# Reading the 384 moving columns of the MLP products as two interleaved halves

## The chip, the cores and the metric

The kernel runs on one core of one Trainium2 chip. The metric is the device time of one execution in microseconds (us), here the median of several runs. A core has a matrix engine (PE, TensorE), whose loads of the stationary operand are shown as PEld, a vector engine (DVE), an activation engine (ACT), a third elementwise engine (POOL, GpSimd), and SP, which issues DMAs.

## What is computed

An attention with random features, then a two-layer MLP with SiLU, then a gated three-matrix MLP, on 2304 tokens of 512 features, all in float32:

```python
def _moe_ref(x, w_in, w_out):                 # 512 -> 2048 -> 512
    h = x @ w_in
    g = h * (1.0 / (1.0 + np.exp(-h)))
    return g @ w_out

def _moe2_ref(x, w_gate, w_val, w_out):       # 512 -> 1536 -> 512
    g = x @ w_gate
    silu = g * (1.0 / (1.0 + np.exp(-g)))
    return (silu * (x @ w_val)) @ w_out

x = attention(q, k, v, omega)                 # (2304, 512)
out = _moe2_ref(_moe_ref(x, w_in, w_out), w_gate, w_val, w_out2)
```

## The kernel before, in words

Activations are kept transposed: features on the 128 partitions, tokens along the free dimension. Tokens are cut into three blocks (`s`, NSB = 3) of two halves of N = 384 tokens each. There are four MLP stages, in this order: up 0 (`w_in`), down 0 (`w_out`), up 1 (`w_gate`, `w_val`), down 1 (`w_out2`). Each is computed with seven block products of a Strassen scheme (`PROD`, `ORDER`) in place of eight; sums and differences of blocks are made by ACT, DVE and POOL. Each float32 operand is split into a high and a low float32r part, and each product is taken as high by high, high by low and low by high, three matmuls.

The up stages run in `up_phase`. Its inner function `products` (line 1085) issues one block product: six matmuls at line 1097, each with a stationary 128x128 piece of a weight (`cut(l, j * P, P)`) and 384 moving columns of an activation block (`cut(r, j * N, N)`), into one PSUM bank `ps[b][:, :N]`. The down stages run in `down_phase`; for each pair of feature blocks it issues twelve matmuls at line 1472, again 128x128 by 384 columns (`b` is the high or low activation piece). The result of a stage is drained from PSUM by ACT (lines 1114, 1138, 1413) and DVE (1155, 1171, 1427), goes through DRAM tensors (`g_d`, `x2_d`), is loaded again, and is split for the next stage (lines 1331, 1335).

Each engine's instructions stand in an order fixed when the program is written: `Op`, `Stream`, `flush` and `need` place work by a planner's cost table, in which a matmul of 384 columns counts as `MM = 0.1735` us. No cost in that table is touched by the change. The attention stage (matmuls at lines 751, 795, 811, 842, 867) comes first; nine matmuls on zeros at line 734 precede it, of the same 128x128 by 384 form as those of the MLPs.

On the host, `kernel` lays out the inputs, launches once, and transposes `out_0` (512 x 2304) at the end.

Of the kernel before, what the change touches and what calls it, by code (L numbers as in the profile page):

```python
# [42 lines left out]
def kernel(  # L43
# [34 lines left out]
    N = 384  # L78
# [20 lines left out]
    ps = [pp.tile([P, 512], F32, name=f"ps{i}") for i in range(8)]  # L99

    def cut(t, o, n):
        return t[:, o : o + n]

    W_AT, T_AT, X_AT = 0, 7168, 10752
    S_AT, C_AT, R_AT, SUM_AT, XR_AT = 0, 3840, 5376, 7424, 8448
# [168 lines left out]
    def need(*keys):  # L274
        for k in keys:
            while k not in T:
                st, o = maker.get(k, (None, None))
                if st is None:
                    u = [o for o in urgent if k in o.outs]
                    if not u:  # L280
                        assert drain(), f"{k} is made nowhere"
                        continue
                    o = u[0]
                need(*o.ins)
                if o.ready() is None:

                    assert drain(), f"{k}: stuck"
                elif k not in T:
                    if st is None:
                        urgent.remove(o)  # L290
                        o.emit()
                    else:
                        while st.q[o.eng][0] is not o:
                            p = st.q[o.eng][0]
                            need(*p.ins)
                            if p.ready() is None:
                                assert drain(), f"{k}: stuck"
                            elif st.q[o.eng][0] is p:
                                st.emit(p)
                        if k not in T and o.ready() is not None:  # L300
                            st.emit(o)

    f_raw = Free("raw", [cut(fa, R_AT + i * 1024, 1024) for i in range(2)])
    f_c = Free("c", [cut(fa, C_AT + i * 512, 512) for i in range(3)])
    f_sum = Free("sum", [cut(fa, SUM_AT, 1024)])
    f_z = Free("z", [])
    f_w = Free("w", [cut(ra, W_AT + i * 1792, 1792) for i in range(6)])
# [757 lines left out]
    def up_phase(m, seq, hook):  # L1067
# [17 lines left out]
        def products(n, p, b, start, stop, extra=()):  # L1085
            i, kind, s = seq[n]
            oa, ob = PROD[p]
            need(("W", kind, i), ("X", m, s, ob), *extra)
            wh, wl = (cut(x, OPA[oa] * 256, 256) for x in W[kind, i])
            xh, xl = X[m, s, ob]  # L1090
            t = clk["PE"]
            for k in [("W", kind, i), ("X", m, s, ob), *extra]:
                t = max(t, T[k] + 0.1)
            c = 0
            for j in range(2):
                for l, r in ((wh, xh), (wh, xl), (wl, xh)):
                    nc.tensor.matmul(  # L1097
                        ps[b][:, :N],
                        cut(l, j * P, P),
                        cut(r, j * N, N),  # L1100
                        start=start and c == 0,
                        stop=stop and c == 5,
                        skip_group_check=True,
                    )
                    c += 1
            clk["PE"] = t + 6 * MM
            T[K("P", n, p)] = clk["PE"]
# [79 lines left out]
        for _, n, p in sorted(slots):  # L1187
# [3 lines left out]
            a, b = ps[A[n % 2]], ps[B[n % 2]]  # L1191
            hook(n, p)
            flush(clk["PE"])
            if p == 1:
                products(n, 1, A[n % 2], True, False, [K("h", n - 2, 0)] if n > 1 else [])
                copy(n, 1, b[:, :N], a[:, :N], "AB", free=[("a", n - 2, 3)])
                if m == 0 and n == 0:
# [117 lines left out]
    def down_phase(m, Wd, hook, gap_until=None):  # L1315
# [78 lines left out]
        BANKS = {1: 0, 2: 0, 5: 2, 3: 2, 6: 4, 7: 4, 4: 6}  # L1394
# [55 lines left out]
        for s in range(NSB):  # L1450
            for p in ORDER:
                for k in range(np_):
                    hook(s, p, k)
                    flush(clk["PE"])
                    keys = [K("hi", s, p, k), K("lo", s, p, k)]
                    keys += [("Wd", m, p, g) for g in {2 * k // 3, (2 * k + 1) // 3}]
                    if k == 0 and p in BEFORE:
                        keys += [K("v", s, BEFORE[p], e) for e in range(2)]
                    if k == 0 and p in (1, 5) and s:
                        keys += [K("v", s - 1, {1: "C11", 5: "C12"}[p], e) for e in range(2)]  # L1460
                    need(*keys)
                    t = clk["PE"]
                    for x in keys:
                        t = max(t, T[x] + 0.1)
                    hi, lo = ops.pop((s, p, k))
                    for j in range(2):
                        i = 2 * k + j
                        wh, wl = (cut(t, (i % 3) * 256, 256) for t in Wd[p, i // 3])
                        h, l = cut(hi, j * N, N), cut(lo, j * N, N)
                        for e in range(2):  # L1470
                            for c, (a, b) in enumerate(((wh, h), (wh, l), (wl, h))):
                                nc.tensor.matmul(  # L1472
                                    ps[BANKS[p] + e][:, :N],
                                    cut(a, e * P, P),
                                    b,
                                    start=p in FIRST and i == 0 and c == 0,
                                    stop=p in LAST and i == fp - 1 and c == 2,
                                    skip_group_check=True,
                                )
                    clk["PE"] = t + 12 * MM  # L1480
                    for t in (hi, lo):
                        n = len(lent)
                        lent[:] = [x for x in lent if x is not t]
                        if len(lent) < n:
                            f_op.give(t)
                        elif t is not gap or (s, p) != gap_until and not gone:
                            f_z.give(t)
                        else:
                            gone.append(t)
                    if (s, p, k) == (*(gap_until or (0, 0)), np_ - 1) and not gone:  # L1490
                        f_z.q = deque(x for x in f_z.q if x[0] is not gap)
                        gone.append(gap)
                    if s == NSB - 1 and (k == np_ - 1):
                        for g in range((fp + 2) // 3):
                            for t in Wd.pop((p, g)):
                                f_op.give(t)
                T[K("P", s, p)] = clk["PE"]
                ended(s, p)
# [191 lines left out]
```

## Time and profile before

| what | value |
|---|---|
| median of 3 runs | 884.25 us |
| lowest and highest run | 883.42 and 886.79 us |
| span of the profiled execution, first to last instruction | 881.1 us |
| PE busy | 866.9 us, 98% of the span |
| PEld busy | 843.1 us, 96% |
| DVE, ACT, POOL busy | 620.3, 546.5, 165.6 us |

The page gives the span of the profiled execution as its only time; the median of the runs is 3.15 us above it, which holds what lies before the first and after the last instruction and the difference from run to run. The busy times overlap. [...]

### The profile page before, as it was taken

The page shows a single profiled execution, that of the slowest core. Times are in us where ns is not written, and L with a number is a line of the kernel's source. Part 1 is how long each engine was busy: PE and PEld are TensorE (multiplying, and loading weights), DVE is VectorE, ACT ScalarE, POOL GpSimd, SP SyncE. Part 2 cuts the span into 40 slices and gives each one's busy share as a digit, 9 for nine tenths or more (in the row PEclk, how much of TensorE's full clock was granted, in tenths as well). Part 3 has the DMA queues.
Part 4 walks back from the last instruction along what each step waited for, and adds up shares of the span by engine and source line. Part 5 has one row for each costly group of instructions (what it writes and reads, how often), then busy time and mean ns, then how long its engine had stood idle before and what let it go on. Part 6 is the DMA issues. An engine that isn't in the chain of part 4 may idle for free.

```text
span 881.1 us, 18161 instructions
## 1 busy us (share of the span) xinstructions
PE 866.9 (98%) x6889; PEld 843.1 (96%) x6889; DVE 620.3 (70%) x1016; ACT 546.5 (62%) x1166; POOL 165.6 (19%) x204
## 2 busy tenths in 40 slices
PE   9999999999999989999999999999999999999998
PEld 7888899999999989999998999999999999999998
DVE  4888877565634895885899898555555538978773
ACT  6999868666667764454466865454545357655552
POOL 0487830054520000000000044131212100000000
PEclk9999999999999999999999999999999999999999
DMA  8589776389999837338315467352525267573502
GB/s 275 180 288 298 229 254 219 132 274 307 304 294 390 290 136 231 110 92 243 97 60 194 157 210 245 113 200 96 198 96 173 78 234 244 171 248 107 181 1 72
DMA packets 110119, 170.08 MB, mean 193 GB/s; under 512 B 9424, under 2 KB 94032, under 8 KB 110032
## 3 DMA queue, kind: packets, MB, share of 16 engines
q1 hardware_dynamic: 109808, 168.69, 58.7%
q8 instruction: 54, 0.88, 0.4%
q10 hardware_dynamic: 224, 0.23, 0.1%
q14 instruction: 33, 0.27, 0.1%
HBM read 107.02 MB, written 61.87 MB: 192 GB/s over the span
## 4 chain that ended last, share of the span: by engine, by line
PE 73%; issue 7%; DVE 7%; DMA 7%; ACT 4%; POOL 2%; SPq 1%; DVEq 0%; ACTq 0%; POOLq 0%
PE ps L1097 32%; PE ps L1472 31%; PE ps L751 4%; DMA g_d<-fa 2%; PE ps L795 2%; POOL fa L376 2%; PE ps L811 2%; DMA wd_out<-fa 1%; PE ps L842 1%; ACT kq L767 1%; DVE ra L423 1%; DVE fa L357 1%; DMA ra<-g_d 1%; DVE ra L1335 1%; DMA fa<-in_moe_w_out 1%
## 5 line engine op out<-in xcount | busy, mean ns | idle before, releaser
L376 POOL TENSOR_TENSOR fa<-fa 128x256 f32<-128x256 f32 x124 | 105.9, 869 | 526.0 <-DVE fa L357 317.3
L1097 PE MATMUL ps<-ra 128*128 128x384 f32 x840 | 156.0, 335 | 1.6 <-ACT ps L1114 1.5
L1097 PE MATMUL ps<-rc,ra 128*128 128x384 f32 x840 | 154.8, 334 | 0.7 <-ACT ps L1114 0.7
L1097 PE MATMUL ps<-rb,ra 128*128 128x384 f32 x840 | 154.7, 334 | 0.5 <-ACT ps L1114 0.5
L1097 PEld LDWEIGHTS ps<-ra 128*128 128x128 f32 x840 | 146.2, 188 | 2.8 <-ACT ps L1114 2.8
L1097 PEld LDWEIGHTS ps<-rc,ra 128*128 128x128 f32 x840 | 146.2, 188 | 1.7 <-ACT ps L1114 1.7
L1097 PEld LDWEIGHTS ps<-rb,ra 128*128 128x128 f32 x840 | 146.3, 188 | 1.1 <-ACT ps L1114 1.1
L1114 ACT ACTIVATE ps<-ps 128x384 f32<-128x384 f32 x180 | 85.8, 476 | 84.5 <-PE ps L1097 75.5
L1171 DVE TENSOR_TENSOR fa<-fa,ps 128x384 f32<-128x384 f32 x120 | 66.2, 552 | 99.7 <-ACT ps L1114 71.7
L1331 ACT ACTIVATE ra<-fa 128x768 fp32r<-128x768 f32 x86 | 72.6, 846 | 68.7 <-PE ps L1472 49.1
L1335 DVE TENSOR_TENSOR ra<-fa,ra 128x768 fp32r<-128x768 f32 x81 | 77.5, 957 | 30.9 <-PE ps L1472 15.0
L1472 PE MATMUL ps<-ra,rb 128*128 128x384 f32 x516 | 95.7, 335 | 2.3 <-DVE ra L1335 2.3
L1472 PEld LDWEIGHTS ps<-ra,rb 128*128 128x128 f32 x516 | 89.8, 188 | 3.5 <-DVE ra L1335 3.4
L1472 PE MATMUL ps<-ra,rc 128*128 128x384 f32 x482 | 89.3, 335 | 1.9 <-DVE ra L1335 1.9
L1472 PE MATMUL ps<-ra 128*128 128x384 f32 x486 | 86.3, 335 | 1.2 <-ACT ra L1331 0.7
L1472 PEld LDWEIGHTS ps<-ra,rc 128*128 128x128 f32 x482 | 83.8, 188 | 3.3 <-DVE ra L1335 3.1
L1472 PEld LDWEIGHTS ps<-ra 128*128 128x128 f32 x486 | 84.3, 188 | 1.9 <-ACT ra L1331 1.0
L767 ACT ACTIVATE kq<-ps,nb 128x128 f32<-128x128 f32 x288 | 79.8, 411 | 9.2 <-DVE nb L765 8.6
L1355 DVE TENSOR_TENSOR fa<-ra,fa 128x768 f32<-128x768 f32 x63 | 60.1, 954 | 2.4 <-DMA ra<-g_d 1.7
L1138 ACT ACTIVATE fa<-fa 128x384 f32<-128x384 f32 x84 | 43.8, 521 | 27.5 <-DVE fa L1171 27.5
L343 ACT ACTIVATE fa<-fa 128x512 f32<-128x512 f32 x65 | 44.1, 679 | 17.8 <-DMA fa<-in_moe_w_in 6.6
L765 DVE TENSOR_REDUCE nb<-ps 128x4 f32<-128x512 f32 x72 | 48.1, 681 | 6.7 <-PE ps L751 3.1
(112 smaller groups left out, 1120.4 us busy)
## 6 DMA issues: line engine op xcount, KB each, us to landing
g_d<-fa SPq DMA_DIRECT2D x168, 192.0 KB, 3.7
fa<-g_d SPq DMA_DIRECT2D x42, 384.0 KB, 4.7
ra<-g_d SPq DMA_DIRECT2D x42, 384.0 KB, 4.1
fa<-in_moe_w_out SPq DMA_DIRECT2D x28, 512.0 KB, 5.2
fa<-in_moe_w_in SPq DMA_DIRECT2D x16, 512.0 KB, 5.0
wd_out<-fa SPq DMA_DIRECT2D x12, 512.0 KB, 3.3
fa<-in_moe_w_gate SPq DMA_DIRECT2D x12, 512.0 KB, 4.0
fa<-in_moe_w_val SPq DMA_DIRECT2D x12, 512.0 KB, 5.4
```

The costliest lines, as they stand in the source:

```text
L343: nc.scalar.activation(c, word(h, 1).bitcast(F32), AF.Prelu, scale=2.0**-112, alpha=-(2.0**32))
L376: f(blk(f"S{n}"), blk(l), blk(r))
L765: nc.vector.reduce_max(nb, x, axis=AX.X, negate=True)
L767: nc.scalar.activation(e[:, g // 2, g % 2, h * M : (h + 1) * M], x[:, g, :], AF.Exp, bias=nb[:, g : g + 1])
L1097: nc.tensor.matmul(ps[b][:, :N], cut(l, j * P, P), cut(r, j * N, N), start=start and c == 0, stop=stop and c == 5, skip_group_check=True,)
L1114: nc.scalar.activation(out() if callable(out) else out, src, AF.Copy)
L1138: nc.scalar.activation(b["t"], src, AF.Silu)
L1171: nc.vector.tensor_add(t, t if in_place else p5[n], ps[bank_][:, :N])
L1331: nc.scalar.activation(ops[s, p, k][0], src(), AF.Copy)
L1335: nc.vector.tensor_sub(l, src(), h.bitcast(F32))
L1355: (nc.gpsimd if eng == "POOL" else nc.vector).tensor_sub(z(PLACE[to]), z(PLACE.get(l, l)), z(PLACE.get(r, r)))
L1472: nc.tensor.matmul(ps[BANKS[p] + e][:, :N], cut(a, e * P, P), b, start=p in FIRST and i == 0 and c == 0, stop=p in LAST and i == fp - 1 an ...
```

## The change

Two access patterns are added, and used in the two places where MLP products are issued. `halves` reads a moving operand of 384 columns as column 0, 192, 1, 193, ..., 191, 383. `woven` writes the 384 result columns as 192 pairs in their order. In the built program the output pattern is one run of 384 neighbouring columns, as before, and the moving pattern is 192 pairs whose two members lie 192 columns (768 bytes) apart. So each of the four stages leaves its tokens interleaved once more than it found them, inside each block of 384, and the host undoes this four times.

```diff
+    def halves(t):
+        return t.rearrange("p (a b) -> p b a", a=2)
+
+    def woven(t):
+        return t.rearrange("p (b a) -> p b a", a=2)
...
                     nc.tensor.matmul(
-                        ps[b][:, :N],
+                        woven(ps[b][:, :N]),
                         cut(l, j * P, P),
-                        cut(r, j * N, N),
+                        halves(cut(r, j * N, N)),
...
                                 nc.tensor.matmul(
-                                    ps[BANKS[p] + e][:, :N],
+                                    woven(ps[BANKS[p] + e][:, :N]),
                                     cut(a, e * P, P),
-                                    b,
+                                    halves(b),
...
-    return np.ascontiguousarray(r.results[0]["out_0"].T)
+    out = r.results[0]["out_0"].reshape(512, 6, 384)
+    for _ in range(4):
+        out = out.reshape(512, 6, 192, 2).swapaxes(2, 3).reshape(512, 6, 384)
+    return np.ascontiguousarray(out.reshape(512, 2304).T)
```

No instruction that does work is added, dropped or moved: the rows of PE, DVE, ACT, POOL and SP stand in the same order in both programs. What differs beside the moving pattern are waits: 9 instructions of DVE and 137 of ACT have another set of semaphores to wait for, nearly always one on ACT's own earlier instructions that comes or goes, and ACT has 45 more instructions that only wait.

## Rows read from the trace of the kernel before

**Rows 1.** The page, busy time by engine, and the granted clock in 40 slices.

```profile
PE 866.9 (98%) x6889; PEld 843.1 (96%) x6889; DVE 620.3 (70%) x1016; ACT 546.5 (62%) x1166; POOL 165.6 (19%) x204
PEclk9999999999999999999999999999999999999999
```

**Rows 2.** Stretches: engines' busy us (and instructions), granted clock, DMA share, GB/s.

```profile
20.00:118.00 98.00, 97.18 (x2231) 83.04 (x2231) 85.42 (x187) 89.79 (x293) 67.94 (x84) 1.00 0.76 241
118.00:878.00 760.00, 751.52 (x4344) 744.66 (x4342) 526.94 (x811) 443.04 (x828) 96.93 (x112) 1.00 0.56 185
```

**Rows 3.** The chain that ended last: shares of the span by line; its last pieces.

```profile
PE 73%; issue 7%; DVE 7%; DMA 7%; ACT 4%; POOL 2%; SPq 1%; DVEq 0%; ACTq 0%; POOLq 0%
...
839.84 37.80 PE ps L1472 x218
877.64 0.02 issue
877.67 0.49 ACT fa L1413
```

**Rows 4.** PE groups of the MLPs: count, busy us, mean ns, idle us before.

```profile
L1097 PE MATMUL ps<-ra 128*128 128x384 f32 x840 | 156.0, 335 | 1.6 <-ACT ps L1114 1.5
L1097 PE MATMUL ps<-rc,ra 128*128 128x384 f32 x840 | 154.8, 334 | 0.7 <-ACT ps L1114 0.7
L1097 PE MATMUL ps<-rb,ra 128*128 128x384 f32 x840 | 154.7, 334 | 0.5 <-ACT ps L1114 0.5
L1472 PE MATMUL ps<-ra,rb 128*128 128x384 f32 x516 | 95.7, 335 | 2.3 <-DVE ra L1335 2.3
L1472 PE MATMUL ps<-ra,rc 128*128 128x384 f32 x482 | 89.3, 335 | 1.9 <-DVE ra L1335 1.9
L1472 PE MATMUL ps<-ra 128*128 128x384 f32 x486 | 86.3, 335 | 1.2 <-ACT ra L1331 0.7 <-DVE ra L1335 0.6
L1472 PE MATMUL ps<-rb,rc 128*128 128x384 f32 x112 | 23.6, 334 | 0.0
L1472 PE MATMUL ps<-rb 128*128 128x384 f32 x96 | 21.3, 334 | 0.0
L1472 PE MATMUL ps<-rb,ra 128*128 128x384 f32 x72 | 13.0, 334 | 0.0
```

**Rows 5.** PE in order of time: start us, length us of each unbroken run, count.

```profile
118.24 1.23 PE L1097 MATMUL ps<-ra 128*128 128x384 f32 x6
...
341.89 18.36 PE L1472 MATMUL ps<-ra,rc 128*128 128x384 f32 x105
...
599.97 4.32 PE L1097 MATMUL ps<-rc,ra 128*128 128x384 f32 x24
```

**Rows 6.** The nine matmuls on zeros, first two and all; durations min, median, max.

```profile
1.32 1.01 PE L734 MATMUL ps<-zero 128*128 128x384 f32 x2 [1.32 <-DVE zero L717]
...
1.32 3.25 PE L734 MATMUL ps<-zero 128*128 128x384 f32 x9 [1.32 <-DVE zero L717]
...
L734 PE MATMUL ps<-zero x9: 522/522/688, 1.3 to 4.0; 128*128 128x384 f32 x9
```

**Rows 7.** ACT and DVE groups: lines 343 and 357 read every second word.

```profile
L343 ACT ACTIVATE fa<-fa 128x512 f32<-128x512 f32 x65 | 44.1, 679 | 17.8 <-DMA fa<-in_moe_w_in 6.6 <-DMA fa<-in_moe_w_gate 3.7 <-DMA fa<-in_moe_w_val 3.0
L410 ACT ACTIVATE ra<-fa 128x512 fp32r<-128x512 f32 x15 | 9.3, 621 | 1.5 <-POOL fa L376 1.5
L357 DVE SCALAR_TENSOR_TENSOR fa<-fa 128x512 uint32<-128x512 uint32 x65 | 48.4, 745 | 0.5
L423 DVE TENSOR_TENSOR ra<-fa,ra 128x512 fp32r<-128x512 f32 x45 | 31.2, 708 | 0.0
```

**Rows 8.** Line 343 by instruction: an ACT instruction that only waits, ns min, median, max.

```profile
L343 ACTq EVENT_SEMAPHORE  x53: 17/17/1830, 51.6 to 676.1; - x53
```

## The prediction

> **What bounds the kernel now.** I read the busy times first. PE is busy for 866.9 of 881.1 us and no other engine for more than 70% [rows 1]. The reader should not stop there, since an average hides stages, so next come the stretches: in the MLP part, from 118 to 878 us, PE is busy for 751.52 of 760 us, DVE for 526.94 and ACT for 443.04, at granted clock 1.00 [rows 2]. The chain of work that ended last says the same for the end: from 839.84 us on it is one run of 218 matmuls of line 1472, and only 0.49 us of ACT stand behind it [rows 3]. So in the MLPs the matmul stream sets the time, and whatever one matmul costs more is paid as often as there are matmuls.
>
> How many are there? Line 1097 has 3 x 840 = 2520, line 1472 has 516 + 482 + 486 + 112 + 96 + 72 = 1764, together 4284 [rows 4]. What does one cost? Not its 334 ns: these overlap. 24 matmuls of line 1097 in a row last 4.32 us, and the last one starts 0.334 us before the end of that, so one step is (4.32 - 0.334) / 23 = 0.1733 us; 105 of line 1472 give (18.36 - 0.335) / 104 = 0.1733 us [rows 4, 5]. 4284 steps of 0.1733 us are 742.4 us, of the 759.4 us from the first MLP matmul at 118.24 to 877.6 us [rows 3, 5]. The remaining 17 us are a few attention matmuls at the start and waits; PE's own idle rows of lines 1097 and 1472 sum to 1.6 + 0.7 + 0.5 + 2.3 + 1.9 + 1.2 = 8.2 us [rows 4].
>
> [...] Each partition thus reads 2.2 float32 words a nanosecond for the moving operand. Nothing else in this trace reads that fast: ACT takes 512 words in 621 ns and DVE in 708 ns, 0.8 and 0.7 words a nanosecond [rows 7].
>
> **The change part by part.** *The moving read* is the whole case. Instructions, order, weights and the output pattern stay; the 384 words come from two places 768 bytes apart, in turn. The trace shows no matmul that reads like this, so I bound its step from both sides.
>
> - Lower bound: nothing changes, 0.1733 us. [...]
> - Upper bound from the nearest row on the other side: the nine matmuls on zeros, same 128x128 by 384 form. The first two end 1.01 us and all nine 3.25 us after the same start, so a step is (3.25 - 1.01) / 7 = 0.320 us [rows 6]. [...] This row gives what a matmul costs when its columns come at 1.2 a nanosecond, for whatever reason.
>
> Which one? My supposition, which no row of before proves, is that the stream today takes two neighbouring words from one access and so lives with half as many accesses as columns. In the new order no two words in a row are neighbours, so each access would serve one word. [...] Against a full-price view stand the rows of line 343 on ACT and 357 on DVE, which read every second word and cost 679 against 621 ns and 745 against 708 ns [rows 7], next to nothing. But those engines ask for under one word a nanosecond, and so need no second word from an access; PE asks for 2.2. I take the upper bound as nearest, and add the 0.0133 us that a step has today beyond its columns, as I see no reason that it should hide: 0.320 + 0.0133 = 0.3333 us. Without that addition the step is 0.320 us, and twice today's step is 0.3466 us; these two are the ends for this case.
>
> [...]
>
> Sum for the MLP stream: 4284 x (0.3333 - 0.1733) = 4284 x 0.160 = 685.4 us more.
>
> *The waits.* ACT and DVE have the same work per matmul and nearly twice the time, so PE's waits for line 1114, 1331 and 1335 should go: 8.2 us less [rows 4]. If they stay, the time is that much higher. What is late next? Nothing: with 760 us of MLP time grown to about 1440, DVE's 526.94 us are 37% of it [rows 2], and the DMA share of 0.56 falls likewise.
>
> *The 45 wait-only instructions on ACT* cost 17 ns each by the median of such a row, 45 x 0.017 = 0.8 us [rows 8], on an engine that is idle for 40% of the MLP part [rows 2]; queued behind them are ACT's copies out of PSUM, for which PE waits at some block products. Under the longer stream I cost them at nothing; without that cover, at most 0.8 us for the instructions themselves. The changed waits are for ACT instructions several places back in ACT's own order, which should be done by then.
>
> *The attention part* up to 118.24 us is not touched. *The host's reordering* is not device time.
>
> **Total.** Against the profiled span: 881.1 + 685.4 - 8.2 = 1558.3 us. The median of the runs is 3.15 us above the span, 884.25 against 881.1; I add that: **1561.5 us**, 77% longer.
>
> **The rivals.**
>
> 1. *The moving read hides the alternation, so nothing changes*: about 884 us, or up to 885 with the ACT waits uncovered. For it: the read pattern returns to the same two places every other word, so a reader that keeps two places open, or fetches far ahead, would need no more accesses than before; each instruction still names its 384 words in one simple pattern. Against it: PE has no slack to hide anything in, 751.52 of 760 us [rows 2], so it must hide all of it. It decides from the point where a step stays below 0.1743 us (0.001 x 4284 = 4.3 us, the 0.5% that a measurement of this kernel can tell from no change). Chance 0.15.
>
> 2. *A small price per word, as on the other engines*: ACT's row has 58 ns more on 512 words, 0.113 ns a word [rows 7]; on 384 words 0.0435 us a step, 186 us in all, so about 1060 us with the waits gone. For it: these are the only rows in which a read with gaps stands beside one without. Against it: the operations compared are not the same (another function on ACT, another opcode on DVE), and these engines read too slowly to need two words at once. Anything between 900 and 1500 us counts here. Chance 0.10.
>
> 3. *The half-fed array loses its clock as well*: if the granted clock fell to its lower level and a column then took two cycles of that, a step would be 2 x 0.320 = 0.640 us, 4284 x 0.4667 = 1999 us more, about 2880 us; any price above 1630 us, such as one full memory wait for each word, counts here. Against the clock: in the attention part, with short matmuls, the granted clock is 1.00 as well [rows 2]. Chance 0.06.
>
> 4. *The change does not do what it says*, because the pattern is merged again into 384 neighbours. The built program shows the output merged and the moving operand not merged, so I give this nothing of its own; it would look like rival 1.
>
> **How the numbers follow.** Half the column rate 0.68, no change 0.15, small price 0.10, worse 0.06, a gain 0.01. The forecast's own range: with a step of 0.320 us, 881.1 + 4284 x 0.1467 - 8.2 + 3.2 = 1505 us; with 0.3466 us and the waits as they are, 881.1 + 742.4 + 3.2 = 1627 us. Leaving out no change, worse and a gain would leave out 0.22, more than 2 in 10, so the range goes down to no change and up to the forecast's own end: **880 to 1630 us**. Faster by over 0.5%: 0.01; within 0.5%: 0.15; slower: 0.84.
>
> **What the profile after would show.** For the forecast: groups of lines 1103 and 1478 (the same matmuls, six lines lower) with runs of 24 that last about 23 x 0.333 + 0.5 = 8.2 us instead of 4.32; the first MLP matmul still at 118 us; the granted clock at 1.00; idle time of PE in the MLP part near zero, and the waits of ACT and DVE for PE grown two- to threefold. Rival 1 would show 4.32 us for such a run; rival 2 about 5.3 us; rival 3 a granted clock at 0.5 in the MLP part or a step above 0.35 us. What would make the prediction wrong is one thing: the rate at which the moving operand can be read out of order. All else is small beside it.

## The result: 31 us faster, with shorter matmul steps

The changed kernel takes 852.92 us (median of 4 runs, 851.53 to 858.19), beside 883.93 us for the kernel before (4 runs, 883.42 to 886.79): a ratio of 0.9655, 95% interval 0.9622 to 0.9688. It is faster, where 1561.5 us was forecast.

The page of the changed kernel, its span and the busy time by engine:

```profile
span 850.5 us, 18213 instructions
PE 822.9 (97%) x6889; PEld 794.7 (93%) x6889; DVE 622.8 (73%) x1016; ACT 551.1 (65%) x1166; POOL 163.5 (19%) x204
```

PE is busy 44 us less than in [rows 1]; ACT and DVE are a little busier. The stretch of the MLPs answers to the second line of [rows 2] (columns: us, then busy us and instructions of PE, PEld, DVE, ACT, POOL, granted clock, DMA share, GB/s):

```profile
118.00:848.00 730.00, 708.47 (x4341) 697.23 (x4339) 529.26 (x811) 448.05 (x828) 95.40 (x112) 1.00 0.59 192
```

The stage is 30 us shorter at the same granted clock, and PE is busy for 97% of it, after 99%. The groups of the MLP products (six lines lower than in [rows 4]), and one unbroken run of 24 in order of time, which answers to the last line of [rows 5]:

```profile
L1103 PE MATMUL ps<-ra 128*128 128x384 f32 x840 | 148.1, 327 | 6.6 <-ACT ps L1120 5.8
L1103 PE MATMUL ps<-rb,ra 128*128 128x384 f32 x840 | 146.7, 327 | 3.0 <-ACT ps L1120 3.0
L1478 PE MATMUL ps<-ra,rb 128*128 128x384 f32 x516 | 90.6, 327 | 3.3 <-DVE ra L1341 3.3
```

```profile
571.33 4.06 PE L1103 MATMUL ps<-rb,ra 128*128 128x384 f32 x24
```

24 matmuls last 4.06 us, so a step is (4.06 - 0.327) / 23 = 0.1623 us, after 0.1733 us: 11 ns less. 4284 x 0.011 = 47.1 us. The kernel gained 31.0, so 16 us came back. Where they came back stands in who waits for whom (us in total, times, longest), first in the changed kernel, then in the kernel before:

```profile
PE ps L1103 <- ACT ps L1120: 11.0, 17, 1.7
PE ps L1478 <- DVE ra L1341: 7.5, 8, 1.9
```

```profile
PE ps L1472 <- DVE ra L1335: 4.7, 6, 1.7
PE ps L1097 <- ACT ps L1114: 2.7, 7, 1.3
```

Such idle time is counted from the end of a matmul, which lies about two steps behind its start, so short waits do not show in it. Counted from start to start in the trace, over the steps that are more than 0.06 us too long, PE lost 15.9 us in the MLPs before and 32.6 us after: 16.7 us more. So what came back is time in which PE waits, and the shorter step itself holds throughout the MLPs.

Two groups beside PE have changed, two steps of the weight conversions, on ACT line 343 in [rows 7], now 349, and on DVE line 357, now 363:

```profile
L349 ACT ACTIVATE fa<-fa 128x512 f32<-128x512 f32 x65 | 54.6, 842 | 22.2 <-DMA fa<-in_moe_w_in 7.7 <-DMA fa<-in_moe_w_val 5.3 <-DMA fa<-in_moe_w_gate 4.3
L363 DVE SCALAR_TENSOR_TENSOR fa<-fa 128x512 uint32<-128x512 uint32 x65 | 55.3, 850 | 0.5
```

842 ns after 679 and 850 after 745, for the same work. Both read every second word; the groups that read neighbours are as before (line 1337 on ACT 841 ns after 846, line 1341 on DVE 955 after 957).

So there were three questions: why the step is shorter, why two groups beside it are slower, and what gave 16 us back.

### The profile page after: what moved, and what is told of

Read it like the earlier page. It is cut to its first block, busy times and chain, and to the rows that moved or that the text cites. A ratio compares the mean times of both kernels' runs of the same rounds, so it can differ in the third digit from the quotient of the medians.

```text
span 850.5 us, 18213 instructions
## 1 busy us (share of the span) xinstructions
PE 822.9 (97%) x6889; PEld 794.7 (93%) x6889; DVE 622.8 (73%) x1016; ACT 551.1 (65%) x1166; POOL 163.5 (19%) x204
## 4 chain that ended last, share of the span: by engine, by line
PE 64%; DMA 11%; issue 9%; DVE 7%; ACT 4%; POOL 3%; SPq 1%; ACTq 0%; DVEq 0%; POOLq 0%
PE ps L1478 27%; PE ps L1103 26%; PE ps L757 4%; POOL fa L382 3%; PE ps L801 3%; DMA ra<-g_d 3%; DMA g_d<-fa 2%; PE ps L817 2%; PE ps L848 2%; DMA wd_out<-fa 2%; DMA fa<-g_d 1%; DVE ra L429 1%; DVE fa L363 1%; DVE ra L1341 1%; DMA rb<-wd_out 1%
## 5 line engine op out<-in xcount | busy, mean ns | idle before, releaser
L1103 PE MATMUL ps<-ra 128*128 128x384 f32 x840 | 148.1, 327 | 6.6 <-ACT ps L1120 5.8
L1103 PE MATMUL ps<-rb,ra 128*128 128x384 f32 x840 | 146.7, 327 | 3.0 <-ACT ps L1120 3.0
L1103 PE MATMUL ps<-rc,ra 128*128 128x384 f32 x840 | 146.2, 327 | 2.1 <-ACT ps L1120 2.1
L1103 PEld LDWEIGHTS ps<-ra 128*128 128x128 f32 x840 | 137.6, 189 | 9.1 <-ACT ps L1120 7.9
L1103 PEld LDWEIGHTS ps<-rb,ra 128*128 128x128 f32 x840 | 137.6, 189 | 4.9 <-ACT ps L1120 4.8
L1103 PEld LDWEIGHTS ps<-rc,ra 128*128 128x128 f32 x840 | 137.7, 189 | 3.6 <-ACT ps L1120 3.6
L1478 PE MATMUL ps<-ra,rb 128*128 128x384 f32 x516 | 90.6, 327 | 3.3 <-DVE ra L1341 3.3
L1478 PEld LDWEIGHTS ps<-ra,rb 128*128 128x128 f32 x516 | 84.5, 189 | 5.1 <-DVE ra L1341 4.7
L1478 PE MATMUL ps<-ra 128*128 128x384 f32 x486 | 81.5, 327 | 3.1 <-DVE ra L1341 2.1
L1478 PEld LDWEIGHTS ps<-ra 128*128 128x128 f32 x486 | 79.2, 189 | 4.2 <-DVE ra L1341 3.1
L349 ACT ACTIVATE fa<-fa 128x512 f32<-128x512 f32 x65 | 54.6, 842 | 22.2 <-DMA fa<-in_moe_w_in 7.7
L363 DVE SCALAR_TENSOR_TENSOR fa<-fa 128x512 uint32<-128x512 uint32 x65 | 55.3, 850 | 0.5
```

Of the source, the lines that this page charges most:

```text
L349: nc.scalar.activation(c, word(h, 1).bitcast(F32), AF.Prelu, scale=2.0**-112, alpha=-(2.0**32))
L363: nc.vector.scalar_tensor_tensor(c, word(h, 0), 29, c, op0=ALU.logical_shift_right, op1=ALU.bitwise_or)
L1103: nc.tensor.matmul(woven(ps[b][:, :N]), cut(l, j * P, P), halves(cut(r, j * N, N)), start=start and c == 0, stop=stop and c == 5, skip_gro ...
L1478: nc.tensor.matmul(woven(ps[BANKS[p] + e][:, :N]), cut(a, e * P, P), halves(b), start=p in FIRST and i == 0 and c == 0, stop=p in LAST and ...
```

## What one step costs: two preludes of matmuls

**m1_forms** puts groups of 24 equal matmuls ahead of the attention, where the other engines are quiet, each with another moving pattern (the edits of the preludes are shown shortened).

```diff
+    MW, MX, R = ra[:, 6144:6272], ra[:, 0:384], 24        # constants
+    for _ in range(R):  # two halves in turn
+        nc.tensor.matmul(ps[0][:, :384].rearrange('p (b a) -> p b a', a=2), MW,
+                         MX.rearrange('p (a b) -> p b a', a=2), start=True, stop=True)
...
+    for _ in range(R):  # every second column
+        nc.tensor.matmul(ps[0][:, :384].rearrange('p (a b) -> p a b', a=2), MW,
+                         MX.rearrange('p (b a) -> p a b', a=2), start=True, stop=True)
```

> The kernel before, with 48 groups of 24 equal matmuls put ahead of the attention (constants, results unused), to read the step of each moving pattern while the other engines are quiet. Known: one row of neighbours 0.1733 us a step, two halves in turn 0.1623 us, 384 columns. Theory A, neighbouring words cost: the step falls with the length of the runs; runs of 96 stay near 0.173, runs of 2 lie between, every stride from 2 up gives 0.162; the excess grows with the number of columns (512: about 0.228 against 0.216). Theory B, the form of the pattern: any pattern that can't be merged into one row avoids a fixed cost, so runs of 96, runs of 2 and all strides give 0.162, and the excess is 0.011 at every column count. Theory C, the next weight load collides with the moving read: with 64 or 32 stationary columns the excess in one row halves or goes to a quarter, at every column count it is the same, and the distance between the halves may matter.

PE in order of time (start us, length us of the group, count). The lines shown are, from above: halves in turn, neighbours, runs of 2 from each half, every second column, every fourth, four parts in turn, eight parts in turn:

```profile
12.84 4.06 PE L744 MATMUL ps<-ra 128*128 128x384 f32 x24
16.73 4.33 PE L746 MATMUL ps<-ra 128*128 128x384 f32 x24
20.90 6.24 PE L748 MATMUL ps<-ra 128*128 128x384 f32 x24
...
48.85 8.47 PE L760 MATMUL ps<-ra 128*128 128x384 f32 x24
...
65.30 8.50 PE L764 MATMUL ps<-ra 128*128 128x384 f32 x24
...
81.41 5.09 PE L768 MATMUL ps<-ra 128*128 128x384 f32 x24
86.33 8.15 PE L770 MATMUL ps<-ra 128*128 128x384 f32 x24
```

From the start of a group to the start of the next, divided by 24 (for bf16 from the length of the group less its last matmul, divided by 23), the steps are:

| moving pattern, 384 columns of float32r | step, ns |
|---|---|
| neighbours | 173.7 |
| two halves in turn, 192 to 2048 words apart (11 distances) | 162.1 to 163.3 |
| runs of 2, 4, 8, 16, 32, 96 from the two halves in turn | 252.9, 191.2, 183.3, 180.4, 179.6, 177.1 |
| every 2nd, 3rd, 4th, 8th column | 345.4, 340.0, 346.3, 325.0 |
| four parts in turn, eight parts in turn | 205.0, 332.1 |
| one column for all 384 | 165.4 |
| neighbours, halves, with 64 stationary columns | 172.9, 162.5 |
| neighbours, halves, with 32 stationary columns | 173.3, 162.5 |
| 512 columns: neighbours, halves | 227.9, 215.8 |
| bf16, 384 columns: neighbours, halves | 162.9, 364 |

Groups of 64 to 256 columns are left out, and so is the first group of neighbours: the granted clock was 0.50 in part of them, and 1.00 in the others. Theory C falls: a stationary operand of a quarter of the columns changes nothing. Theory B falls: runs of 96 can't be merged into one row either, and cost 177.1 ns. Theory A is right that runs of 96 stay near the price of neighbours, and wrong on runs of 2 (252.9 ns, above both ends) and on every stride (twice the price, where 0.162 was expected). None of the three was right as a whole. And every second column does cost about what I had forecast for the halves (345.4 against 333 ns).

**m3_forms** asks the next question in the same manner: does the price go by the step from one column at an even place to the next (and the same at odd places)? Its patterns are such a step s (`hstep2` to `hstep8`), a distance d between the two places, and blocks of 2k columns whose halves are taken in turn (`blk2` to `blk96`, by their k).

```diff
+    def at(t, *dims):
+        return bass.AP(tensor=t.tensor, offset=t.offset, ap=[list(t.ap[0]), *[list(d) for d in dims]])
+    # hstep s: words 0, 2048, s, 2048 + s, ...
+        nc.tensor.matmul(..., MW, at(ra, (s, 192), (2048, 2)), start=True, stop=True)
+    # d: words 0, d, 1, 1 + d, ...
+        nc.tensor.matmul(..., MW, at(ra, (1, 192), (d, 2)), start=True, stop=True)
+    # blk k: blocks of 2k columns, their halves in turn
+        nc.tensor.matmul(..., MW, at(ra, (2 * k, 192 // k), (1, k), (k, 2)), start=True, stop=True)
```

> The kernel before with 39 groups of 24 equal matmuls ahead of the attention (constants, results unused), to tell why two halves in turn run at 0.162 us a step, four parts in turn at 0.205, eight at 0.33 and every fixed stride at 0.33 to 0.35. [...] Rival V: what counts is that the pattern has two places only, each with step one; then hstep2 already costs 0.3 or more, and blk2, blk4 cost as runs of 2 or 4 did (0.25, 0.19). [...]

In order of time: step 2, 3, 4 and 8 at even and at odd places, then neighbours with each pair swapped, then blocks of 4, 8 and 16 columns:

```profile
72.63 4.33 PE L776 MATMUL ps<-ra 128*128 128x384 f32 x24
76.80 6.40 PE L778 MATMUL ps<-ra 128*128 128x384 f32 x24
83.03 8.34 PE L780 MATMUL ps<-ra 128*128 128x384 f32 x24
91.18 8.50 PE L782 MATMUL ps<-ra 128*128 128x384 f32 x24
99.51 4.34 PE L784 MATMUL ps<-ra 128*128 128x384 f32 x24
103.69 4.32 PE L786 MATMUL ps<-ra 128*128 128x384 f32 x24
107.85 4.06 PE L788 MATMUL ps<-ra 128*128 128x384 f32 x24
111.75 4.06 PE L790 MATMUL ps<-ra 128*128 128x384 f32 x24
```

Two of its bf16 groups, halves in turn and every second column; a matmul lasts 0.526 us in the first and 0.331 us in the second, so the steps are (8.90 - 0.526) / 23 = 0.364 us and (4.24 - 0.331) / 23 = 0.170 us:

```profile
147.45 8.90 PE L808 MATMUL ps<-ra 128*128 128x384 bf16 x24
165.09 4.24 PE L814 MATMUL ps<-ra 128*128 128x384 bf16 x24
```

With a step of 1, 2, 3, 4, 8 words at even and at odd places the matmul costs 162.5, 173.8, 259.6, 339.6, 347.1 ns. From two words to four the price is nearly in proportion to the step, 86.9, 86.5 and 84.9 ns for each word of it; from four to eight it hardly rises. From one to two it is not in proportion: 162.5 ns is far above 87. An estimate from the clock says what may bind there. At granted clock 0.50 a step of neighbours takes 0.320 us (m2_contend), and so does one of blocks of 16 columns (blk8), so there the order makes no difference; half of that, 160 ns, would be what 384 columns cost by themselves at 1.00. By these rows **neighbours are the case of step 2**: the even places read words 0, 2, 4, the odd places 1, 3, 5, and they cost 173.7 ns, as hstep2 does with 173.8. That would be the whole excess of 11 ns. Two halves in turn are the case of step 1. Other widths agree: neighbours of 320, 448 and 512 columns cost 146.3, 202.9 and 227.9 ns, halves in turn 135.8, 189.6 and 215.8 ns, 10.5 to 13.3 ns less. Blocks of 8 columns and more are step 1 for at least four words in a row: 162.5 ns. Blocks of 4 are two words in a row: 173.3 ns. The distance between the two places does not matter, from 0 to 160 words: 162.5 to 162.9 ns in 13 groups, so the excess is not from the two places lying next to each other. Nor is it from the pattern being one single row: hstep2, swapped pairs and blocks of 4 are no single row, and cost 173.8, 174.2 and 173.3 ns.

Rival V falls: hstep2 costs 173.8 ns, not 300 or more, and blocks of 4 and of 8 cost 173.3 and 162.5 ns, not 253 and 191. That the step at even and at odd places sets the price is a reading that fits most of the rows; why it should, no run shows. Four things do not fit it: four parts in turn and runs of 2 go to a far word at each column of the even places and should cost about 346 ns, as steps of 4 and 8 do, and cost 205 and 253; every eighth column and eight parts in turn cost 325 and 332 for the same 346; neighbours that start at word 1 cost 178 to 179 ns in both preludes, at word 3 only 173.3; and runs of 4 to 96 cost 3 to 18 ns more than neighbours. For bf16 the reading is wrong: halves in turn cost 364 ns in both preludes, pairs of the two halves in turn 203.7, runs of four 167.5, every second column 170. The first two are about 1 ns for each change of place (384 and 192 of them); that was not followed up.

**every_second** takes the other order into the whole kernel, to see whether a prelude's step can be carried over.

```diff
     def halves(t):
-        return t.rearrange("p (a b) -> p b a", a=2)
+        return t.rearrange("p (b a) -> p a b", a=2)
     def woven(t):
-        return t.rearrange("p (b a) -> p b a", a=2)
+        return t.rearrange("p (a b) -> p a b", a=2)
```

The result is still written as one row of 384 neighbours, and the host undoes the new order.

> The changed kernel with another order of the 384 moving columns: 0, 2, 4, ..., 382, 1, 3, ... . From the group of matmuls that read so (0.345 us a step): 4284 x (0.345 - 0.173) = 737 us more than the kernel before, less some 8 us of waits, about 1610 us. If what the prelude showed does not hold inside the kernel, the time stays within 10% of 853 us.

1605.84 us in one run. The run of 24 in it, in order of time, and the MLP stretch:

```profile
901.50 8.50 PE L1103 MATMUL ps<-ra 128*128 128x384 f32 x24
```

```profile
118.00:1600.00 1482.00, 1481.83 (x4347) 893.01 (x4346) 526.22 (x813) 452.36 (x828) 89.67 (x112) 1.00 0.29 95
```

A matmul of this group lasts 0.529 us, so a step is (8.50 - 0.529) / 23 = 0.3466 us, with PE without a gap and the granted clock unchanged at half the rate of columns. The 1605.84 us are within 0.3% of the 1610 that the prelude's price gave, and all that the prediction said of a stream at half rate (waits gone, clock kept) is right for this order.

## What is slower beside PE

**m2_contend** lets ACT and DVE run the same operations, ten of each, while PE is idle, and beside three streams of 400 matmuls.

```diff
+    for _ in range(400):  # PE, halves in turn
+        nc.tensor.matmul(woven(ps[0][:, :384]), MW, halves(MX), start=True, stop=True)
+    for _ in range(10):  # ACT, every second word
+        nc.scalar.activation(AO, RF[:, 2048:3072].rearrange('p (c w) -> p c w', w=2)[:, :, 0], AF.Copy)
```

> The kernel before, with a prelude in which ACT and DVE run the same ten operations of each kind (512 words read as neighbours, every second, every fourth, two halves in turn) four times: PE idle, PE on 400 matmuls in one row, on 400 with halves in turn, on 400 with every fourth column. Theory G1, PE's order of reading slows reads with gaps on ACT and DVE: ACT's every-second read goes from about 0.64 (idle) and 0.67 (one row) to about 0.85 us with halves in turn, and reads of neighbours stay within 2%. Theory G2, the slower ACT line of the kernel after has another cause: all ACT and DVE rows agree within 3% under the three matmul streams.

ACT's ten reads of every second word (ns min/median/max), beside neighbours, halves in turn, and every fourth column:

```profile
L769 ACT ACTIVATE fa<-fa x10: 676/687/697, 43.0 to 49.5; 128x512 f32<-128x512 f32 x10
```

```profile
L795 ACT ACTIVATE fa<-fa x10: 931/977/1010, 123.0 to 132.1; 128x512 f32<-128x512 f32 x10
```

```profile
L821 ACT ACTIVATE fa<-fa x10: 690/698/711, 188.4 to 194.9; 128x512 f32<-128x512 f32 x10
```

With PE idle the median is 673 ns. The row beside neighbours is a weak one, since that stream began slowly, at 0.320 us a step and a granted clock of 0.50 (the columns are those of the MLP stretch above):

```profile
43.20:49.30 6.10, 6.06 (x19) 6.09 (x20) 5.65 (x14) 5.85 (x9) 0.00 (x0) 0.50 0.00 0
```

The next prelude repeats it beside neighbours at full rate, and has 678 ns. DVE's reads of every second word go from 428 to 557 ns, every fourth on ACT from 1138 to 1532; reads of neighbours stay (ACT 630 and 632, DVE 427 and 427), and so do reads in ACT's own halves-in-turn order (760 and 756). G1 holds, with 977 ns even above the 0.85 us that it gave: beside matmuls that read two halves in turn, reads with gaps on ACT and DVE are slower (977 and 557 ns), beside neighbours (678 ns) and every fourth column (698 ns) ACT's are not.

**m4_contend** changes the distance of the two places, at the same step of 0.1625 us, with blocks.

```diff
+    for _ in range(300):  # PE, blocks of 2k columns, halves in turn, k = 192, 4, 8, 32, 96
+        nc.tensor.matmul(..., MW, MX.rearrange('p (c a b) -> p c b a', a=2, b=k), start=True, stop=True)
```

> As the earlier prelude with ACT and DVE beside streams of matmuls, now with the two places 192, 4, 8, 32 and 96 columns apart inside blocks, with halves whose words are two apart, and with neighbours again. Theory: what slows reads with gaps on ACT and DVE is that PE takes its columns from two far places; at 4 or 8 columns apart ACT's every-second read falls back to about 0.69 us, at 32 and 96 it stays near 0.98. [...]

ACT's reads of every second word, at k = 192, 8, and 96, beside halves whose words are two apart, and beside neighbours:

```profile
L787 ACT ACTIVATE fa<-fa x10: 829/886/998, 115.1 to 123.4; 128x512 f32<-128x512 f32 x10
```

```profile
L831 ACT ACTIVATE fa<-fa x10: 673/680/687, 213.2 to 219.6; 128x512 f32<-128x512 f32 x10
```

```profile
L875 ACT ACTIVATE fa<-fa x10: 687/694/702, 311.5 to 318.0; 128x512 f32<-128x512 f32 x10
```

```profile
L897 ACT ACTIVATE fa<-fa x10: 671/676/689, 360.6 to 367.0; 128x512 f32<-128x512 f32 x10
```

```profile
L919 ACT ACTIVATE fa<-fa x10: 671/678/687, 409.5 to 415.8; 128x512 f32<-128x512 f32 x10
```

At k = 4 and 32 it is 680 and 700 ns. So it isn't the pace of PE alone, but 32 and 96 columns do no harm either, against what I expected. Of the distances tried at 0.1625 us a step only 192 does; the size of the harm is not fixed, 886 ns here and 977 in m2_contend for the same order. The halves whose words are two apart lie 384 columns apart and do no harm, but run at 0.173 us a step, so they do not tell distance from pace. Why 192 is not settled, and no distance above 192 was tried at full rate.

**blk8** makes a kernel of it, beside **after_again**, the changed kernel once more.

```diff
     def halves(t):
-        return t.rearrange("p (a b) -> p b a", a=2)
+        return t.rearrange("p (c a b) -> p c b a", a=2, b=8)
     def woven(t):
-        return t.rearrange("p (b a) -> p b a", a=2)
+        return t.rearrange("p (c b a) -> p c b a", a=2, b=8)
```

The host undoes this order.

> The changed kernel, but the two places are 8 columns apart, inside blocks of 16 (0, 8, 1, 9, ..., 7, 15, 16, 24, ...); the host puts the output back accordingly. From the preludes the step stays 0.1625 us and reads with gaps on ACT and DVE are no longer slowed. Theory: line 349 on ACT is back at about 0.68 us and line 363 at 0.75, and the time is 2 to 5 us below the changed kernel, 848 to 851 us. Rival: with the other engines' real work beside it the order makes no difference; 853 us, and line 349 stays at 0.84.

> The changed kernel itself on the same chip, beside the one with blocks of 16: 852 to 854 us, line 349 at 0.84 us.

850.82 us (ratio to the kernel before 0.9623, interval 0.961 to 0.9637), and 854.51 us for the changed kernel in the same comparison (0.9667, 0.9653 to 0.9681): 3.7 us less, the intervals apart; the changed kernel came 0.5 us above what was expected. Line 349 in both, first blocks of 16 columns:

```profile
L349 ACT ACTIVATE fa<-fa 128x512 f32<-128x512 f32 x65 | 44.4, 685 | 20.6 <-POOL fa L382 6.1 <-DMA fa<-in_moe_w_in 5.0 <-DMA fa<-in_moe_w_gate 4.0
```

```profile
L349 ACT ACTIVATE fa<-fa 128x512 f32<-128x512 f32 x65 | 54.8, 845 | 20.5 <-DMA fa<-in_moe_w_in 6.7 <-DMA fa<-in_moe_w_val 4.9 <-DMA fa<-in_moe_w_gate 4.1
```

Line 363 is at 759 ns, after 838 in the changed kernel beside it. So this kernel beats the kernel before and the changed one.

## What gave 16 us back

The stages, from the first matmul of each to the first of the next (the last to its end), read from PE in order of time, and what 11 ns a step would give:

| stage | matmuls | before, us | after, us | gained | 11 ns a step | given back |
|---|---|---|---|---|---|---|
| up 0 | 1008 | 180.3 | 177.4 | 2.9 | 11.1 | 8.2 |
| down 0 | 1008 | 182.2 | 174.4 | 7.8 | 11.1 | 3.3 |
| up 1 | 1512 | 264.8 | 252.1 | 12.7 | 16.6 | 3.9 |
| down 1 | 756 | 132.1 | 125.4 | 6.7 | 8.3 | 1.6 |

Half of it is in up 0. The four stages hold 30.1 of the 31 us.

**up_only** and **down_only** make the change at one of the two lines.

```diff
     # up_only: line 1097 as in the change, line 1472 as before, the host undoes two stages; down_only the other way round
```

> Halves in turn in the up stages alone (line 1097), the down stages as before. By the step alone 2520 x 0.011 = 27.7 us less than before. Theory: ACT's slower conversion of weights, which lies in the up stages, gives 12 us of that back, so about 16 us less (868 us). Rival: the waits that came back belong to the down stages as well, and this kernel keeps nearly all, 25 us or more.

> Halves in turn in the down stages alone (line 1472). By the step alone 1764 x 0.011 = 19.4 us less. Theory: no weight conversions run beside the down stages, so nearly all stays, about 15 us less (869 us), and the two parts add to the 31 us of the whole change. Rival: the down stages wait for their own splits of activations, and under 8 us stay.

868.22 us (ratio 0.9821, 0.98 to 0.9841) and 869.16 us (0.9832, 0.9814 to 0.985): 15.6 and 14.7 us less, together 30.2 of the 31. The parts add, and the up stages give back 12 of their 27.7 us, as expected; that ACT's slower conversion is the cause of it is not shown by this, and the next pair speaks against it. down_only gives back 4.7 of 19.4, as expected.

**nogap_before** and **nogap_after** take the reads with gaps away: the conversions read neighbours, and ACT's first step multiplies by zero, so that the weights come out as almost zero.

```diff
-            return b["r", h].bitcast(U32).rearrange("p (c w) -> p c w", w=2)[:, :, w]
+            return b["r", h].bitcast(U32)[:, w * 512 : (w + 1) * 512]
...
-                nc.scalar.activation(c, word(h, 1).bitcast(F32), AF.Prelu, scale=2.0**-112, alpha=-(2.0**32))
+                nc.scalar.activation(c, word(h, 1), AF.Prelu, scale=0.0, alpha=0.0)
```

> The kernel before, but ACT and DVE read the raw weight words as neighbours in place of every second one, and ACT's first step multiplies by zero, so that the weights come out as almost zero and the output is not the reference's; instructions, sizes and transfers are the same. Control for the next: 0 to 6 us below the kernel before (65 reads of ACT are some 50 ns shorter).

> The same in the changed kernel: no read with gaps is left on ACT and DVE in the weight conversions, and weights come out as almost zero. Theory: of the 16 us that the change gives back, the conversions that the new read order slows take about half; this kernel is 38 us or more below nogap_before, where the change alone brought 31. Rival: what is given back is the latency of ACT's and DVE's steps between block products, which the shorter matmul stream no longer covers; then the difference between the two stays at 31 us, within 3.

883.33 us (0.9997, 0.9988 to 1.0007) and 849.48 us (0.9613, 0.9598 to 0.9627): 33.9 us apart, where the change brought 31; the rival, 31 within 3, holds. The change's own interval is 3 us wide to each side, so the difference of 2.9 us is not clear of noise by itself; blk8, which takes the slowed reads away in another way, has 3.7 us clear of it. So the slowed reads cost about 3 us of the 16, not half: the theory falls.

**replan** tells the planner of the shorter step.

```diff
-    MM = 0.1735
+    MM = 0.164
```

> The changed kernel, with the planner told that a matmul of 384 columns takes 0.164 us in place of 0.1735; this moves work of ACT, DVE, POOL and SP to other places among the matmuls, and changes nothing else. Theory: part of the 13 us that come back without the slower conversions is an order planned for slower matmuls; then 3 to 8 us less than the changed kernel, 845 to 850 us. Rival: the steps of ACT and DVE between block products are themselves too long for the shorter stream; then 853 us, within 3.

853.19 us (0.9658, 0.9622 to 0.9693): no different from the changed kernel, and above the 845 to 850 of the theory. In the traces 245 of ACT's 1166 places and 225 of DVE's 1016 hold another instruction than before. So this re-planned order does not bring the time back; other orders were not tried.

**shortcopy_before** and **shortcopy_blk8** cut the copies from PSUM to PSUM, for which PE waits in the up stages, to a quarter of their columns, so part of each intermediate sum is missing.

```diff
-                nc.scalar.activation(out() if callable(out) else out, src, AF.Copy)
+                if callable(out):
+                    nc.scalar.activation(out(), src, AF.Copy)
+                else:
+                    nc.scalar.activation(out[:, :96], src[:, :96], AF.Copy)
```

> The kernel before with ACT's copies from one PSUM bank to another in the up stages (180 of line 1114) cut to 96 of 384 columns, so the output is not the reference's. Each such copy becomes some 0.23 us shorter. PE waits for them for 2.7 us in all before; 0 to 6 us less than before.

> The same cut in the kernel with blocks of 16 columns. Theory: what the faster stream gives back is the length of these copies between block products, which it no longer covers; then this kernel is 5 us or more further below its own form without the cut than the kernel before is below its, and PE's waits for line 1120 fall from 11 us to under 5. Rival: the copies wait behind ACT's other work in its queue, or the weights come late; then the cut brings no more than 2 us beyond what it brings before.

882.56 us (0.9988, 0.9979 to 0.9997) and 849.57 us (0.9614, 0.9599 to 0.9629): 1.0 and 1.3 us less than their forms without the cut. A copy lasts 236 ns after 476, and in blk8 PE's waits for them go from 9.1 to 7.0 us only, not to under 5. So the copies' own length isn't it, and the rival is left, that they come late because of what stands before them. What that is can be seen in ACT's order of time just before one of PE's waits in up 0 (blk8; in brackets the idle time before an instruction and who ended it):

```profile
245.38 0.67 ACT L349 ACTIVATE fa<-fa 128x512 f32<-128x512 f32 x1 [1.15 <-POOL fa L382]
246.59 0.68 ACT L349 ACTIVATE fa<-fa 128x512 f32<-128x512 f32 x1 [0.54 <-DMA fa<-in_moe_w_val]
247.17 0.48 ACT L1144 ACTIVATE fa<-ps 128x384 f32<-128x384 f32 x1
247.54 0.52 ACT L1144 ACTIVATE fa<-fa 128x384 f32<-128x384 f32 x1
247.96 0.49 ACT L1120 ACTIVATE ps<-ps 128x384 f32<-128x384 f32 x1
```

ACT stands idle for 1.7 us ahead of two weight conversions, one waiting for POOL to leave a buffer, one for raw weights to land; behind them in its queue stand the drains, and the copy that PE waits for (PE starts again at 248.49 us).

**light_before** and **light_after** test that: as the nogap pair, weights almost zero, and each load of raw weights brings a quarter of its bytes. Two fills of buffers with zeros on POOL, early in the attention part, come with it, since the short loads leave the rest of the buffers unwritten.

```diff
-                nc.sync.dma_start(out=r.bitcast(U32), in_=wsrc[kind][i, h])
+                nc.sync.dma_start(out=r.bitcast(U32)[:, :256], in_=wsrc[kind][i, h][:, :256])
...
+    nc.gpsimd.memset(fa[:, R_AT : R_AT + 2048], 0.0)
+    nc.gpsimd.memset(fa[:, XR_AT : XR_AT + 1536], 0.0)
```

> As nogap_before (weights come out as almost zero, the output is not the reference's), and each load of raw weights brings a quarter of its bytes: 128 KB in place of 512 KB in each of the 80 loads of the conversions. Control: in the kernel before PE waits only 1 us in all of up 0, so 0 to 3 us below nogap_before's 883.3 us.

> The same cut in the changed kernel; to be held against nogap_after (849.5 us). Theory: in the up stages ACT stands in its queue before a weight conversion that waits for its load or for the buffer behind it, and the drains that PE waits for stand behind it; with short loads up 0 takes 170 us or less in place of 176, and the time is 4 to 10 us below nogap_after. Rival: ACT's waits there are for POOL and DVE, or its own work is too long; then the time stays within 2 us of nogap_after.

880.19 us (0.9958, 0.9944 to 0.9972) and 842.86 us (0.9537, 0.9521 to 0.9554). Against the nogap pair the short loads bring 3.1 us before and 6.6 us after. ACT's first conversion step in nogap_after and in light_after, and up 0 with short loads:

```profile
L349 ACT ACTIVATE fa<-fa 128x512 f32<-128x512 uint32 x65 | 41.2, 636 | 23.6 <-DMA fa<-in_moe_w_in 7.6 <-POOL fa L382 5.3 <-DMA fa<-in_moe_w_gate 4.6
```

```profile
L349 ACT ACTIVATE fa<-fa 128x512 f32<-128x512 uint32 x65 | 40.8, 630 | 0.0
```

```profile
118.00:288.00 170.00, 167.86 (x1070) 166.77 (x1069) 109.67 (x195) 126.94 (x273) 43.99 (x48) 1.00 0.70 239
```

ACT no longer idles ahead of a conversion (0.0 us, after 23.6 in nogap_after), and up 0 takes 169.6 us in place of 175.9; before the change it goes from 180.4 to 177.9. Both numbers of the theory came, and PE's waits for the copies of line 1120 (1122 there) go from 8.8 us in nogap_after to 4.7. The short loads also take 27 of 170 MB from all transfers, so other transfers land sooner as well (the stores to g_d in 2.5 us after 3.6 in nogap_after); the pair does not tell this apart from ACT's queue. The light pair is 37.3 us apart.

So of the 47.1 us, 31.0 are kept, 2.9 go to the slowed reads, 3.4 to transfers of weights that hold ACT's queue, and 9.8 are still unexplained; each of these parts can be off by 2 to 3 us (after_again kept 29.1). In the light pair 2.8, 3.9, 3.2 and 0.8 us are still given back in up 0, down 0, up 1 and down 1. Part of this stands in waits that all the changed kernels keep: for splits of activations on DVE (line 1341) at both ends of down 0, and once for 1.5 us for line 1120 in up 1. These were seen in the traces and not tested.

One more part is in the clock. In the traces of blk8 and light_after the granted clock falls to 0.50 in down 0, right behind those waits at its start (blk8: us, then PE, PEld, DVE, ACT, POOL, granted clock, DMA share, GB/s):

```profile
308.00:320.00 12.00, 8.73 (x51) 7.89 (x50) 11.97 (x15) 8.22 (x12) 0.00 (x0) 1.00 0.26 98
320.00:323.40 3.40, 3.40 (x13) 3.40 (x12) 2.63 (x4) 0.84 (x1) 0.00 (x0) 0.50 0.00 0
```

Ten steps take 0.320 us there in place of 0.1625, which is 1.6 us. In the trace of the changed kernel the same waits pass without it. Over whole executions the mean granted clock is 0.995 to 0.998 in 19 of 33 executions of the kernels whose down stages run at the shorter step, and 0.999 or 1.0 in all recorded ones of the kernels whose down stages are as before. So executions of the former may often lose time in this way; that was not tested.

## The prediction, point by point

- *What bounds the kernel* was right: the matmul stream. A change of 11 ns a step moved the whole, and at 347 ns a step the kernel grew as the sum said.
- *The step that failed* is the moving read. The prediction supposed that two neighbouring words are taken from one access, and that in the new order each access serves one word; 4284 x 0.160 = 685.4 us more. Measured: 4284 x 0.011 = 47.1 us less. In the preludes neighbours are not the cheapest order but the last one before the price rises steeply: step 2 at even and at odd places costs 173.8 ns, step 3 costs 259.6, and the new order, step 1, costs 162.5. These prices are measured; how many words one access serves, no run shows.
- *Room for a gain* was there, though no row of before told which order would use it. The prediction's sum carries 0.0133 us of each step along as what a step has beyond its columns, and gives a gain 1 in 100. No run shows that term. What the runs showed in its place are steps of 0.1733 us for neighbours and 0.1623 us for the halves at granted clock 1.00, and of 0.320 us at 0.50 (m2_contend, blk8); half of 0.320 us, 0.160, is an estimate of the columns alone. Of the 13.3 ns above that estimate, which every one of 4284 instructions paid, the change removed 11.
- *The nearest row* was wrongly chosen: by what the runs show, the nine matmuls on zeros told the price of a step at a granted clock of 0.50, not of a read. In m2_contend matmuls that read neighbours take the same 0.320 us while the granted clock is 0.50, and 0.173 us once it is 1.00; the trace of before has no record of the clock ahead of 7.4 us, so the 1.00 that is shown beside the zeros is no measurement. That a time near the forecast exists, every second column with 1606 us, owes nothing to this row: its step of 0.347 us came at granted clock 1.00, so the agreement is luck.
- *Rival 1* (nothing changes) had the right doubt: going to the same two places every other word cost nothing (0.1623 us a step after 0.1733). *Rival 2* took the rows of lines 343 and 357 as a price for PE; what happened is the reverse, these lines became slower because of PE, and no part of the prediction had that. *Rival 3*: in the changed kernel's MLP stretch and in that of every_second, at half the rate, the granted clock was 1.00; the 3.4 us at 0.50 in the traces of blk8 and light_after stand behind PE's waits and cost 1.6 us.
- *The waits* went the other way: PE's idle rows grew from 8.2 to about 20 us, since the stream got shorter; such waits took back 16 of the 47.1 us, and the cause of 9.8 of them stays open. "Nothing is late next" held only for the longer stream; for a shorter one ACT's drains and DVE's splits were next.
- *The 45 wait-only instructions, the first MLP matmul* (117.7 us after 118.2) and *the host's reordering* cost nothing that can be seen.

## What to carry to other kernels

When the busiest engine pays the same step thousands of times (4284 here), measure what other reading orders cost; neighbours need not be the cheapest. For float32r moving operands, try taking two parts in turn, with at least four neighbouring words in each (blocks of 8 columns or more): 162.5 in place of 173.5 ns for 384 columns here, and measure it anew for bf16, where two halves in turn cost 364 ns and neighbours 162.9. And after the busiest engine gets faster, look at queues whose instructions run in order: ACT idled 1.7 us ahead of two weight conversions in blk8, with drains and a copy that PE waited for behind them. Shorter transfers brought 3.1 us before the change and 6.6 us after.

## What the hardware showed that I had not expected

- A matmul of 384 columns that reads two halves in turn costs 162.5 ns with float32r and 364 ns with bf16; with every second column it is the other way round, 345 ns and 170 ns.
- A stream of matmuls can slow reads on ACT and DVE: every second word on ACT from 678 to 886 ns, in another run to 977, when the two places are 192 columns apart, but not at 4, 8, 32 or 96 (680 to 700 ns).
- The granted clock stayed at 1.00 through 1480 us of matmuls at half the rate of columns (every_second), but fell to 0.50 for 3.4 us behind a stretch of 12 us in which PE was busy for 8.73 us (blk8).
